# LSH attention with a token-mixing layer on one core: the order of issue as an explicit list

## The chip, the cores and the metric

One core of one Trainium2 chip runs the whole program. The metric is device time in microseconds (us). Five instruction streams run beside each other: PE (matrix multiply), DVE (VectorE), ACT (ScalarE), POOL (GpSimd) and SP, which here only issues DMAs. Each stream runs its instructions strictly in the order in which the program issued them, and waits on semaphores where it needs another stream's result.

## The reference

Attention with a hash mask comes first, and a token-mixing layer is put on its output:

```python
q_bucket = sum((q @ proj > 0) * 2**k)          # 6 hash bits, the same for k
scores   = where(q_bucket == k_bucket, q @ k.T / 8, -1e9)
attn     = exp(scores - rowmax); attn /= sum(attn) + 1e-9
x        = attn @ v                            # 4 batches, 8 heads, 768 tokens, 64 wide
theta    = x @ w_theta                         # x is now 4 x 768 x 512
y        = w_tok_r @ (x * cos(theta)) + w_tok_i @ (x * sin(theta))
u        = x + y
out      = u + relu(u @ w_ch)
```

Inputs are float32, and the three weight pairs come as float64.

## The kernel before

The kernel is cut into 3,785 small operations. An operation is a Python closure that issues a few instructions on one stream; it is made by `op(name, prio, alts, deps, slots)`, where `alts` names the streams that may run it, with a price in ns each. All matrix products are made of float16 halves (a high and a low part), so many operations exist only to split a tile: `qkh`/`qkl` (L643, L645, L649) for q and k, `p1`/`p2` (L879, L885) for the exponentials, `zh`/`zl` (L1095, L1097, L1101) for the rotated values, `xh`/`xl` (L1007, L1009, L1013) for x and u before they are turned by a DMA transpose (`xturn`, L1017).

For every head: `qkload` (SP) brings q and k, `qksq`, `qksum`, `qksc` find a scale, `qkh` and `qkl` split, `bits` (PE) and `sign` (DVE) make the hash rows, `assemble` and `assbits` (SP) copy the parts into the operands `qt` and `kt`. `qmax` (PE, tile sq) multiplies them once to find row maxima, which `vmax` (DVE, L793, tile mc) reads out of one of two PSUM banks; `vboth`, `mtr`, `row`, `put` write the maxima back into `qt`. Then `st` (PE) makes the masked scores, `pf` (ACT, L873) the exponentials, `p1` and `p2` the halves, and `pv` (PE, tile po) multiplies with v; `recip` and `norm` (L928, L934) write x.

For every batch, once its heads are done: six tiles of `xh`, `xl`, `xturn` and four `proj` on PE (tile ps_th), `turns`, `rest`, `mag`, then `trig` (ACT), `zf`, `zh`, `zl`; 72 `y` operations on PE (tile py); then for each of six token tiles `u`, `xh`, `xl`, `xturn`, four `proj` (tile ps_r), `relu`, `fin` (L1142) and `store` (SP, L1146). The weights are prepared beside the first batch (`wload`, `wlow`, `whigh`, `wmul` and others). The work of one batch's token mixing is interleaved with the next batch's attention; the last batch's stands alone at the end.

What sets the order: `issue_all()` (L117) sorts the operations by a rank (`prio` plus an offset per name and batch in `OFF`), hands out buffer slots by rank, and then runs a list scheduler. It keeps a simulated time per stream from the prices, takes the ready operation of the lowest rank for each idle stream, holds a stream back for an operation of a lower rank that is about to be ready (`HOLD`, `AHEAD`), and models the matrix clock, the DMA wire and the memory port that DVE and POOL share. Where `alts` has two streams, the one that is idle first in the simulation takes the operation. All of this happens when the program is built; the chip sees the resulting order on each stream alone.

Of the kernel before, what the change touches and what calls it, by code (L numbers as in the profile page):

```python
# [34 lines left out]
def lsh_attention_moe_kernel(ctx: ExitStack, tc: tile.TileContext, q, k, v, proj, w_theta, w_tok_r, w_tok_i, w_ch, aff, out):  # L35
# [46 lines left out]
    WINDOW = 3413  # L82
    SAME = {"PE": 0, "ACT": 120, "DVE": 115, "POOL": 160}
    START = {"PE": 1000, "ACT": 1900, "DVE": 1600, "POOL": 4300, "SP": 500}
    STREAM = {"xtr": 0.5, "wtr": 0.5, "mtr": 0.3, "vall": 0.3, "vmean": 0.5, "pv": 0.83, "y": 1.0, "proj": 0.97}
    FULLNS = 244
    LAT = {"PE": 220, "ACT": 120, "DVE": 115, "POOL": 140}
    SHARED = {"p1", "p2", "zf", "zh", "zl", "mag", "wlow", "whigh", "wmul", "wl", "vv2", "qkh", "qkl", "xh", "xl", "fin"}
    SHORT = {"pv", "xtr", "wtr", "mtr", "vall", "vmean", "bits"}
    FOUR = {"proj"}  # L90

# [25 lines left out]
    def issue_all():  # L117
        left = {}
        rng = random.Random(SEED)
        for i, o in enumerate(ops):  # L120
            o.key = (round(o.prio + JIT * rng.random(), 4), i)
            for sl in o.slots:
                left.setdefault(sl, []).append(o)

        free, done, open_, tickets = dict(FREE), set(), {}, {}

        def run(o):
            if o in done:
                return
            if o in open_:  # L130
                raise RuntimeError("no order for " + o.name)
            open_[o] = True
            for d in sorted(o.deps, key=lambda d: d.key):
                run(d)
            while True:
                need = {}
                for sl in o.slots:
                    if not sl.held:
                        need[sl.pool] = need.get(sl.pool, 0) + 1
                short = [p for p, n in need.items() if free[p] < n]  # L140
                if not short:
                    break
                held = [x for x in left if x.held and x.pool == short[0] and x not in o.slots]
                x = min(held, key=lambda x: max(u.key for u in left[x]))
                for u in sorted(left[x], key=lambda u: u.key):
                    run(u)
            for sl in o.slots:
                if not sl.held:
                    sl.held = True
                    free[sl.pool] -= 1  # L150
                    sl.rank = tickets[sl.pool] = tickets.get(sl.pool, -1) + 1
            done.add(o)
            del open_[o]
            for sl in o.slots:
                left[sl].remove(o)
                if not left[sl]:
                    free[sl.pool] += 1
                    del left[sl]

        for o in sorted(ops, key=lambda o: o.key):  # L160
            run(o)

        free = {p: list(range(n)) for p, n in FREE.items()}
        given = {p: set() for p in FREE}
        head = {p: 0 for p in FREE}
        busy = dict(START)
        wire = 0
        port = [0, 0]
        table = None
        succ = {o: [] for o in ops}  # L170
        avail = {e: [] for e in START}
        soon = {e: [] for e in START}
        for o in ops:
            for sl in o.slots:
                sl.held = False
            o.n = o.unissued = len(o.deps)
            o.at = 0
            for d in o.deps:
                succ[d].append(o)
            if not o.n:  # L180
                for e in o.alts:
                    avail[e].append(o)

        tail_pe = None

        def key(o, e):
            if e == "PE" and tail_pe in SHORT and o.name in FOUR:
                return (o.key[0] + PEN, o.key[1])
            return o.key

        def can(o):
            need = {}
            for sl in o.slots:
                if not sl.held:
                    if sl.rank - head[sl.pool] >= WIN.get(sl.pool, 1):
                        return False
                    need[sl.pool] = need.get(sl.pool, 0) + 1
            return all(len(free[p]) >= n for p, n in need.items())

        used, seen, warm = {}, 0, False  # L200

        def pace(t, dur, part):
            nonlocal seen, warm
            while (seen + 1) * WINDOW <= t:
                share = used.get(seen, 0) / WINDOW
                warm = share >= 0.75 or (warm and share > 0.43)
                seen += 1
            dur *= 1 if warm else 2
            a = t
            while a < t + dur:  # L210
                b_ = min(t + dur, (a // WINDOW + 1) * WINDOW)
                used[a // WINDOW] = used.get(a // WINDOW, 0) + (b_ - a) * part
                a = b_
            return dur

        events = [(t_, 0, []) for t_ in sorted(START.values())]
        now, todo, tick = 0, len(ops), 0
        while todo:
            progress = False
            for e in START:  # L220
                if busy[e] > now:
                    continue
                best = None
                for o in avail[e]:
                    k_ = key(o, e)
                    if best is not None and k_ >= best:
                        continue
                    end = now + (HOLD * o.alts[e][0] if e != "SP" else 0)
                    if any(x.at < end and key(x, e)[0] + AHEAD < k_[0] for x in soon[e]):
                        continue  # L230
                    if can(o):
                        best, pick = k_, o
                if best is None:
                    continue
                o = pick
                for a in o.alts:
                    avail[a].remove(o)
                for sl in o.slots:
                    if not sl.held:
                        p = sl.pool  # L240
                        sl.held = True
                        sl.idx = free[p].pop(0)
                        given[p].add(sl.rank)
                        while head[p] in given[p]:
                            given[p].remove(head[p])
                            head[p] += 1
                dur, fn = o.alts[e]
                lat = LAT.get(e, 0)
                if e == "PE":
                    if tail_pe in SHORT and o.name in FOUR:  # L250
                        dur += 80
                    tail_pe = o.name
                    dur = pace(now, dur, STREAM.get(o.name, 0.9))
                elif e == "DVE" and o.name in SHARED:
                    port[0] = max(now, port[1]) + dur
                    dur = port[0] - now
                elif e == "POOL":
                    port[1] = max(now, port[0]) + dur
                    dur = port[1] - now
                elif e == "SP":  # L260
                    t_ = now
                    for hold, size in dur:
                        t_ += 25 + hold
                        wire = max(wire, t_ + 650) + max(size / 360, 60)
                    dur = t_ - now
                    lat = wire + 1050 - t_
                if o.table is not None and o.table != table:
                    dur += 1280
                    table = o.table
                fn()  # L270
                busy[e] = now + dur
                if TRACE is not None:
                    TRACE.append((e, o.name, o.phase, now, dur))
                tick += 1
                same = [c for c in succ[o] if e != "SP" and list(c.alts) == [e]]
                o.same = same
                heapq.heappush(events, (now + dur + lat, tick, o))
# [11 lines left out]
            if progress:  # L289
                continue  # L290
# [1046 lines left out]
```

## Time and profile before

| | |
|---|---|
| runs | 761.12, 762.28, 764.10 us; median 762.28 |
| profiled execution | 763.9 us, span 762.1 us (first to last instruction) |
| busy PE / DVE / ACT / POOL | 705.0 / 582.8 / 550.2 / 409.4 us |
| mean granted TensorE clock | 0.986 of 2.4 GHz |

The span is 1.8 us shorter than the time of the same execution; the rest lies before the first and behind the last instruction. Busy time of PE counts overlapping matmuls once, so a PE that is busy is not always at its full rate. A wait is given as the stream and tile that waited and the one whose event ended it.

### The profile page before, as it was taken

What the parts mean: (1) busy time and instruction counts of PE and PEld (TensorE: products, weight loads), DVE (VectorE), ACT (ScalarE), POOL (GpSimd) and SP (SyncE); (2) the same over time, 40 slices, a digit from 0 to 9 for tenths busy, and PEclk for the clock granted to TensorE, in tenths of its full rate; (3) what the DMA queues carried; (4) which work ended last, traced back from release to release, by engine and by line L of the source; (5) the groups of instructions that cost most, each with busy time, mean ns of one, the idle gap of its engine ahead of it and who ended that gap; (6) DMA issues with size and microseconds to landing.
All of it is one profiled execution on the core that took longest, in us unless ns stands there. A gap on an engine that the chain in (4) does not pass through costs nothing.

```text
span 762.1 us, 17202 instructions
## 1 busy us (share of the span) xinstructions
PE 705.0 (93%) x6516; PEld 417.1 (55%) x6516; DVE 582.8 (76%) x1083; ACT 550.2 (72%) x970; POOL 409.4 (54%) x363
## 2 busy tenths in 40 slices
PE   3689999898899999989999999999999999989997
PEld 1266768674456545555555655565556555544443
DVE  6989988997999885887998755799988655468321
ACT  6478887788997667788896676788996655868111
POOL 3052451634776637776569666686579555733000
PEclk9699999999999999999999999999999999999999
DMA  6265534467103427435403332435204321151212
GB/s 221 86 193 195 164 98 135 94 169 150 40 15 103 111 53 160 118 95 112 77 25 84 92 93 67 125 86 139 64 25 101 80 62 32 29 98 28 56 33 78
DMA packets 85955, 72.09 MB, mean 95 GB/s; under 512 B 58144, under 2 KB 75632, under 8 KB 85872
## 3 DMA queue, kind: packets, MB, share of 16 engines
q1 hardware_dynamic: 85872, 70.99, 36.9%
q8 instruction: 51, 0.84, 0.5%
q14 instruction: 32, 0.26, 0.1%
HBM read 32.51 MB, written 6.29 MB: 51 GB/s over the span
## 4 chain that ended last, share of the span: by engine, by line
PE 54%; DVE 23%; ACT 9%; DMA 7%; issue 4%; POOL 2%; SPq 0%; DVEq 0%; ACTq 0%; POOLq 0%
PE py L79 20%; PE st L79 9%; PE po L79 9%; DVE mc L793 7%; PE ps_r L79 7%; PE sq L79 4%; PE ps_th L79 3%; DMA t_x<-s_x 2%; ACT pf L873 2%; ACT p L879 1%; POOL p L885 1%; DVE hl L649 1%; DMA w_th<-in_moe_w_theta_dram 1%; DMA t_u<-s_u 1%; DVE wf_t L394 1%
## 5 line engine op out<-in xcount | busy, mean ns | idle before, releaser
L885 POOL TENSOR_TENSOR p<-pf,p 128x512 f16<-128x512 f32 x252 | 315.6, 1276 | 190.0 <-ACT p L879 120.9
L793 DVE TENSOR_REDUCE mc<-sq 128x1 f32<-128x512 f32 (+1 forms) x288 | 187.6, 681 | 42.7 <-PE sq L79 41.9
L79 PE MATMUL py<-z,wtk 128*128 128x512 f16 x864 | 211.6, 379 | 1.0 <-POOL z L1101 0.6
L873 ACT ACTIVATE pf<-st 128x512 f32<-128x512 f32 x288 | 163.2, 592 | 58.3 <-PE st L79 45.3
L79 PE MATMUL st<-qt,kt 98*128 98x256 f16 (+3 forms) x768 | 167.4, 328 | 4.2 <-ACT pf L873 2.4
L879 ACT ACTIVATE p<-pf 128x512 f16<-128x512 f32 x252 | 151.0, 629 | 8.6 <-PE po L79 6.8
L79 PEld LDWEIGHTS <-p 128*128 128x128 f16 x3024 | 123.0, 98 | 40.5 <-issue 4.8
L79 PE MATMUL po<-vv,p 128*128 128x65 f16 x3024 | 132.9, 194 | 2.1 <-POOL p L885 1.6
L79 PEld LDWEIGHTS <-wtk 128*128 128x128 f16 x864 | 81.5, 98 | 87.2 <-issue 3.7
L79 PE MATMUL sq<-kt,qt 108*128 108x256 f16 (+1 forms) x384 | 105.0, 338 | 23.0 <-DVE mc L793 17.4
L79 PEld LDWEIGHTS <-kt 108*128 108x128 f16 (+1 forms) x768 | 70.9, 100 | 44.1 <-issue 12.4
L79 PE MATMUL ps_th<-wth,t_x 128*128 128x512 f16 x288 | 66.7, 379 | 5.2 <-DMA t_x<-s_x 5.2
L79 PE MATMUL ps_r<-wch,t_u 128*128 128x512 f16 x288 | 67.6, 379 | 2.7 <-DMA t_u<-s_u 2.3
L1101 POOL TENSOR_TENSOR z<-f,z 128x512 f16<-128x512 f32 x34 | 47.1, 1399 | 41.9 <-ACT z L1095 40.3
L79 PEld LDWEIGHTS <-qt 108*128 108x128 f16 x384 | 36.4, 102 | 57.7 <-issue 26.5
L1090 DVE SCALAR_TENSOR_TENSOR f<-x,zsc,z 128x512 f32<-128x512 f32 x48 | 53.1, 1143 | 2.2 <-ACT z L1078 1.2
L79 PEld LDWEIGHTS <-t_x 128*128 128x128 f16 x288 | 27.4, 98 | 38.7 <-DMA t_x<-s_x 7.5
L79 PEld LDWEIGHTS <-t_u 128*128 128x128 f16 x288 | 27.7, 98 | 35.6 <-DMA t_u<-s_u 3.3
L1129 DVE SCALAR_TENSOR_TENSOR x<-py,sw,x 128x512 f32<-128x512 f32 x24 | 17.9, 747 | 38.0 <-PE py L79 38.0
L1007 ACT ACTIVATE s_u<-x,su 128x512 f16<-128x512 f32 x18 | 13.0, 720 | 42.8 <-DVE x L1129 42.3
L649 DVE SCALAR_TENSOR_TENSOR hl<-raw,sc,hl 128x768 f16<-128x768 f32 x32 | 39.4, 1243 | 0.1
L79 PE MATMUL po<-vw,pf 128*128 128x65 f32 x288 | 36.9, 277 | 1.2 <-ACT pf L873 1.1
(163 smaller groups left out, 845.5 us busy)
## 6 DMA issues: line engine op xcount, KB each, us to landing
raw<-in_q_dram SPq DMA_DIRECT2D x16, 384.0 KB
raw<-in_k_dram SPq DMA_DIRECT2D x16, 384.0 KB
vb<-in_v_dram SPq DMA_DIRECT2D x16, 384.0 KB
out_dram<-x SPq DMA_DIRECT2D x24, 256.0 KB
qt<-hl SPq DMA_DIRECT2D x31, 192.0 KB
kt<-hl SPq DMA_DIRECT2D x31, 192.0 KB
w_t<-in_moe_w_tok_r_dram SPq DMA_DIRECT2D x6, 768.0 KB
w_t<-in_moe_w_tok_i_dram SPq DMA_DIRECT2D x6, 768.0 KB
```

The source lines that it names most:

```text
L79: PE.matmul(out_, l, r, start=start, stop=stop, skip_group_check=True)
L394: DVE.scalar_tensor_tensor(fu, t["hi"], 3, fu, ALU.logical_shift_left, ALU.bitwise_xor)
L649: DVE.scalar_tensor_tensor(t["hl"][:, 1, i], t["raw", i], t["sc"][:, 2 + i : 3 + i], t["hl"][:, 0, i], ALU.mult, ALU.subtract)
L793: DVE.tensor_reduce(col()[:, cs], u["sq"], AX.X, ALU.max)
L873: ACT.activation(wide("pf", spf, F32), u["st"], AF.Exp, scale=1.0 / (UNIT * math.sqrt(D)))
L879: ACT.activation(o_, u["pf"], AF.Copy)
L885: return lambda: eng.tensor_tensor(wide("p2", sp2, F16), u["pf"], u["p1"], ALU.subtract)
L1007: ACT.activation(u["s"][:, 0], src(), AF.Copy, scale=sc())
L1090: DVE.scalar_tensor_tensor(u["f"], tl[b][:, tt], zsc[:, b : b + 1], t["zw"][r][:, tt], ALU.mult, ALU.mult)
L1101: return lambda: eng.tensor_tensor(t["z"][r, 1][:, tt], u["f"], t["z"][r, 0][:, tt], ALU.subtract)
L1129: DVE.scalar_tensor_tensor(tl[b][:, to], res["py"], t["sw"][:, to : to + 1], tl[b][:, to], ALU.mult, ALU.add)
```

## The change

`issue_all()` no longer sorts or schedules. It goes through one list, `ORDER`, of 3,785 tokens, and issues the operations in just that order; `SLOTS` gives the buffer copy of each of the 2,010 slots. The ranks, `OFF`, the window and hold constants and the cost model are gone. Twenty or so prices in `alts` are changed too, but nothing reads a price any more.

```diff
     def issue_all():
-        left = {}
...
-        for o in sorted(ops, key=lambda o: o.key):
-            run(o)
...
+        seen = []
+        for o in ops:
             for sl in o.slots:
                 if not sl.held:
                     sl.held = True
...
+                    seen.append(sl)
+        for sl, c in zip(seen, SLOTS):
+            sl.idx = int(c)
+        done = set()
+        for line in ORDER.split():
+            e, x = line[0], int(line[1:], 36)
+            o = ops[x]
+            if not done.issuperset(o.deps):
+                raise RuntimeError("order of " + o.name)
             done.add(o)
...
+            o.alts[ENGINES[e]][1]()
...
-    proj_ready = op("pst", QK0, on("DVE", 700, split_proj), [cload])
+    proj_ready = op("pst", QK0, on("DVE", 1450, split_proj), [cload])
...
+ENGINES = {"P": "PE", "A": "ACT", "D": "DVE", "G": "POOL", "S": "SP"}
...
+P61 A9n D65 D1w P9q P66 A62 S9y P68 A1x D9r P9w D69 A9s D67 P6c A9u D9t P6a D6b Sdr D6d P6e A9z D9x P6g D6f Sa8 D6h P6i P6k D6j Ads D6l P6u
...
+P2uh P2vw P2vx P2vj P2vy D2vk P2vz D2uz A2vl P2w0 A2ui D2vm P2w1 P2w2 P2ts P2tt P2tu P2w3 A2tv S2v0 P2wi G2tw P2w4 S2ok S2p7 P2wj G2uj S2vn
+P2w5 P2wk P2wl P2v1 P2wm P2wn P2w6 P2wo D2w7 P2wp D2w8 P2wq P2wr P2ws P2wt P2v2 D2wu P2v3 D2wv P2v4 D2w9 P2vo D2ww S2wa P2vp P2vq P2vr A2vs
+S2wx A2v5 P2wb G2vt S2qh P2wc S2na P2wd S2vu P2we S2uk S2pu P2wy A2wf P2wz D2wg P2x0 D2v6 P2x1 S2v7 S2tx A2x2 S2wh D2x3 S2x4
```

A token is a stream's letter and the number of an operation, to base 36, in the order in which the program makes the operations. `A9u` is operation 354, the `qkh` of the second pair of heads, on ACT; `S2x4` is the last, 3784, a `store`.

The list is not the order that the old scheduler gives. Set beside the order in which the instructions stand in the trace of before, it keeps every operation and every buffer copy, but few operations keep their place:

| stream | operations before | in the list | places moved: median, nine in ten within, most |
|---|---|---|---|
| PE | 1460 | 1460 | 2, 8, 32 |
| DVE | 876 | 900 | 1, 5, 57 |
| ACT | 861 | 852 | 1, 5, 30 |
| POOL | 323 | 308 | 0, 1, 5 |
| SP | 265 | 265 | 1, 5, 32 |

Operations that change the stream: 21 `zl` and two `wmul` from POOL to DVE; 8 `zh`, 8 `xh`, 3 `mag` and 3 `qkh` from ACT to DVE; 4 `fin` from POOL to DVE. The other way 7 `qkh`, 5 `xh` and one `mag` go from DVE to ACT, and 10 `fin`, one `wmul` and one `zl` from DVE to POOL. On SP, nine stores are issued behind the last `xturn` (S2qh, S2na, S2vu, S2uk, S2pu, S2v7, S2tx, S2wh, S2x4); before, three were.

## Rows read from the trace of the kernel before

**Rows 1.** The page's first part: busy time of each engine, share of the span, instructions.
```profile
PE 705.0 (93%) x6516; PEld 417.1 (55%) x6516; DVE 582.8 (76%) x1083; ACT 550.2 (72%) x970; POOL 409.4 (54%) x363
```
**Rows 2.** Busy time of each engine by stage. Columns: stretch in us, its length, then busy us and instructions of PE, PE's weight loads, DVE, ACT and POOL, the granted clock, the busy share of the DMA engines, and GB/s.
```profile
0.00:17.00 17.00, 3.78 (x14) 1.54 (x15) 10.11 (x36) 11.50 (x16) 7.56 (x28) 1.00 0.71 230
17.00:50.00 33.00, 24.45 (x195) 12.71 (x196) 29.37 (x63) 21.43 (x39) 10.64 (x9) 0.79 0.48 139
50.00:165.00 115.00, 107.59 (x1120) 83.74 (x1119) 106.33 (x217) 91.23 (x172) 41.26 (x34) 1.00 0.47 137
165.00:220.00 55.00, 48.29 (x379) 24.84 (x378) 48.02 (x83) 49.23 (x82) 33.11 (x27) 1.00 0.43 94
220.00:300.00 80.00, 77.78 (x724) 44.25 (x723) 64.11 (x120) 56.73 (x114) 49.86 (x43) 1.00 0.40 95
300.00:340.00 40.00, 36.33 (x431) 22.40 (x428) 33.70 (x74) 32.11 (x61) 31.07 (x28) 1.00 0.42 111
340.00:390.00 50.00, 47.39 (x455) 27.47 (x455) 43.98 (x75) 42.03 (x70) 33.20 (x27) 0.97 0.38 80
390.00:500.00 110.00, 109.76 (x1092) 63.48 (x1089) 79.94 (x147) 79.05 (x144) 74.47 (x64) 1.00 0.35 89
500.00:545.00 45.00, 42.14 (x428) 25.36 (x425) 41.69 (x72) 40.77 (x70) 28.43 (x25) 0.96 0.48 110
545.00:660.00 115.00, 114.67 (x1142) 66.34 (x1141) 75.07 (x132) 81.51 (x144) 77.12 (x66) 1.00 0.22 54
660.00:695.00 35.00, 30.69 (x278) 17.16 (x277) 25.50 (x40) 27.23 (x42) 16.75 (x14) 1.00 0.36 68
695.00:757.60 62.60, 62.07 (x287) 27.81 (x285) 24.32 (x32) 16.73 (x25) 5.89 (x4) 1.00 0.19 47
757.60:762.10 4.50, 0.04 (x1) 0.00 (x0) 0.69 (x1) 0.69 (x1) 0.00 (x0) 0.86 0.15 58
```
**Rows 3.** What PE waited for over the whole span: waiting tile and line, what ended the wait, us in total, times, longest.
```profile
PE sq L79 <- DVE mc L793: 17.4, 34, 1.7
PE ps_th L79 <- DMA t_x<-s_x: 5.2, 5, 1.6
PE ps_r L79 <- DMA t_u<-s_u: 2.3, 2, 1.8
PE po L79 <- DVE x L934: 1.7, 1, 1.7
```
**Rows 4.** The page's chain of waits that ended last, by engine.
```profile
PE 54%; DVE 23%; ACT 9%; DMA 7%; issue 4%; POOL 2%; SPq 0%; DVEq 0%; ACTq 0%; POOLq 0%
```
**Rows 5.** PE's waits in one stretch each: 17 to 165 us, 165 to 220 us, 300 to 390 us (two rows), 660 to 695 us.
```profile
PE sq L79 <- DVE mc L793: 10.7, 17, 1.7
...
PE ps_th L79 <- DMA t_x<-s_x: 2.7, 2, 1.6
...
PE sq L79 <- DVE mc L793: 3.2, 8, 0.9
PE pmx L806 <- DVE mx L802: 1.7, 1, 1.7
...
PE ps_th L79 <- DMA t_x<-s_x: 2.1, 2, 1.5
```
**Rows 6.** Durations of operations that change the stream: from the groups by shape (count, busy us, mean ns, idle before), and from the answers on L1101 and on the tile x (count, min/median/max ns).
```profile
L645 DVE TENSOR_SCALAR hl<-raw,sc 128x768 f16<-128x768 f32 x11 | 8.3, 766 | 0.2
L1101 POOL TENSOR_TENSOR z<-f,z x34: 1155/1463/1617, 194.3 to 704.4; 128x512 f16<-128x512 f32 x34
L1101 DVE TENSOR_TENSOR z<-f,z x14: 692/997/1643, 195.3 to 707.3; 128x512 f16<-128x512 f32 x14
L1142 DVE TENSOR_TENSOR x<-rl,x x18: 679/693/1641, 283.3 to 758.5; 128x512 f32<-128x512 f32 x18
L1009 DVE TENSOR_SCALAR s_x<-x,zsc x10: 473/480/1382, 165.0 to 685.0; 128x512 f16<-128x512 f32 x10
L408 DVE TENSOR_TENSOR wf_ch<-wf_ch,wg_ch 128x256 f32<-128x256 f32 x3 | 3.0, 1000 | 1.3 <-ACT wf_ch L401 1.3
```
**Rows 7.** SP's stream in order of time: start, length and what it issued.
```profile
168.84 0.39 SPq L632 DMA_DIRECT2D raw<-in_k_dram  x1
169.31 2.21 SPq L1017 DMA_TRANSPOSE t_x<-s_x  x1
...
175.90 1.27 SPq L1017 DMA_TRANSPOSE t_x<-s_x  x1
```
**Rows 8.** DVE's stream in order of time, between 300 and 390 us (two rows) and between 660 and 695 us (a row with the idle time before it).
```profile
328.36 0.68 DVE L1142 TENSOR_TENSOR x<-rl,x 128x512 f32<-128x512 f32 x1
...
333.83 1.56 DVE L645 TENSOR_SCALAR hl<-raw,sc 128x768 f16<-128x768 f32 x1
...
670.57 0.18 DVE L928 RECIPROCAL rc<-po 128x4 f32<-128x4 f32 x1 [0.77 <-PE po L79]
```
**Rows 9.** The tail in order of time, and the last stretch (columns as in rows 2).
```profile
755.88 3.63 SPq L1146 DMA_DIRECT2D out_dram<-x  x2
...
758.46 0.69 DVE L1142 TENSOR_TENSOR x<-rl,x 128x512 f32<-128x512 f32 x1 [2.60 <-ACT rl L1139]
...
752.00:762.10 10.10, 5.11 (x23) 1.98 (x21) 2.08 (x3) 1.85 (x3) 0.00 (x0) 0.94 0.35 104
```

More of the change, by code (lines that the diff above doesn't have):

```diff
@@ L79, in mm @@
         PE.matmul(out_, l, r, start=start, stop=stop, skip_group_check=True)
[L82 to L90, printed above, removed]
     class Slot:
@@ L117, in issue_all @@
     def issue_all():
-        left = {}
[L119 to L146, printed above, removed]
+        seen = []
+        for o in ops:
             for sl in o.slots:
@@ L149, in run @@
                     sl.held = True
-                    free[sl.pool] -= 1
-                    sl.rank = tickets[sl.pool] = tickets.get(sl.pool, -1) + 1
-            done.add(o)
[L153 to L158, printed above, removed]
-        for o in sorted(ops, key=lambda o: o.key):
-            run(o)
-        free = {p: list(range(n)) for p, n in FREE.items()}
@@ L164, in issue_all @@
[L164 to L277, printed above, removed]
-                heapq.heappush(events, (now + dur, -tick, []))
-                if same:
-                    heapq.heappush(events, (now + dur + SAME[e], tick + 0.5, same))
-                for c in succ[o]:
-                    c.unissued -= 1
-                    c.at = max(c.at, now + dur + (SAME[e] if c in same else lat))
-                    if not c.unissued and len(c.alts) == 1:
-                        for a in c.alts:
-                            soon[a].append(c)
-                progress = True
-                todo -= 1
-            if progress:
-                continue
-            if not events:
-                raise RuntimeError("no order of issue: " + ", ".join(o.name for e in avail for o in avail[e])[:2000])
-            now = events[0][0]
-            while events and events[0][0] <= now:
-                _, _, o = heapq.heappop(events)
-                if isinstance(o, list):
-                    nexts = o
-                else:
-                    for sl in o.slots:
-                        sl.users -= 1
-                        if not sl.users:
-                            free[sl.pool].append(sl.idx)
-                    nexts = [c for c in succ[o] if c not in o.same]
-                for c in nexts:
-                    c.n -= 1
-                    if not c.n:
-                        for a in c.alts:
-                            avail[a].append(c)
-                            if c in soon[a]:
-                                soon[a].remove(c)
@@ L444, in prep_weight @@
         a = op("wall", last_, on("PE", 60, total), [a], [sa])
[L445 removed]
+        r = op("wcsc", last_, on("DVE", 620, lambda: root_scale(u["pa"], csc[nm], cinv[nm])), [a], [sa])
         for c in range(NC):
@@ L589, in prep_v @@
         r = op("vload", prio + LV0, on("SP", [(450, 2 * S * D * 4)], load), slots=[svb])
-        r = op("vsq", prio, on("ACT", 900, squares), [r], [svb, sv] + sw_)
+        r = op("vsq", prio, on("ACT", 950, squares), [r], [svb, sv] + sw_)
         r = op("vall", prio, on("PE", 60, total), [r], [svb, sa])
-        r = op("vscale", prio, on("DVE", 520, scale), [r], [sa])
+        r = op("vscale", prio, on("DVE", 630, scale), [r], [sa])
         vready[b].append(r)
-        last_ = a = op("vv1", prio, on("ACT", 960 if n_ == 1 else 830, high), [r], [svb, sv] + sw_)
+        last_ = a = op("vv1", prio, on("ACT", 1030 if n_ == 1 else 830, high), [r], [svb, sv] + sw_)
         if n_:
@@ L676, in prep_qk @@
         r = op("qksum", pr, on("PE", 60, total), sq, [sa, ssc])
-        r = op("qksc", pr, on("DVE", 850, scale), [r], [sa, ssc])
+        r = op("qksc", pr, on("DVE", 1260, scale), [r], [sa, ssc])
         for i, sn, high, low in parts:
@@ L978, in moe @@
         alltk = [o for w in wready["tk"] for o in w]
-        st0 = op("moe", G + at("TH0", b) - 0.5, on("DVE", 800 + 300, start), ([] if b == 0 else alltk) + vready[b] + wready["th"], sz)
+        st0 = op("moe", G + at("TH0", b) - 0.5, on("DVE", 2500 if b else 800, start), ([] if b == 0 else alltk) + vready[b] + wready["th"], sz)
         srow, st1 = [], st0
@@ L983, in moe @@
         if b == 0:
-            st1 = op("ssum", G + at("Y0", 0), on("DVE", 600, sums), [st0] + alltk)
-        st2 = op("sback", G + at("Y0", b), on("DVE", 300, back), [st1] + wready["ch"])
+            st1 = op("ssum", G + at("Y0", 0), on("DVE", 750, sums), [st0] + alltk)
+        st2 = op("sback", G + at("Y0", b), on("DVE", 400, back), [st1] + wready["ch"])
         cnt = [0]
@@ L1062, in mag_a @@
                     ACT.activation(t["zw"][0][:, tt], t["zw"][1][:, tt], AF.Abs)
-                a = op("turns", prio, on("ACT", 495, turns), [pe, st0], [sm_, s1])
-                d = op("rest", prio, on("DVE", 600, rest), [a, st0], [sm_, s1] + sz)
+                a = op("turns", prio, on("ACT", 590, turns), [pe, st0], [sm_, s1])
+                d = op("rest", prio, on("DVE", 650, rest), [a, st0], [sm_, s1] + sz)
                 angles.append((d, op("mag", prio, {"DVE": (335, mag), "ACT": (520, mag_a)}, [d], sz)))
@@ L1079, in go @@
                     ACT.activation(s_, s_, AF.Sin, scale=t["ns"])
-                tr = op("trig", prio, on("ACT", 220 + 844 * (t1 - t0), go), ang, sz, table="trig")
+                tr = op("trig", prio, on("ACT", 480 + 855 * (t1 - t0), go), ang, sz, table="trig")
                 for tt in range(t0, t1):
@@ L1206 @@
 GR = 0
-PEN = 2.584
 GR1 = 2
```

177 lines of the change are left out of this document (154 added, 23 removed), and 38 rows, old and new, of the table OFF.

## The prediction

> **What bounds the kernel now.** I began with the page's busy line: PE is busy for 705.0 of 762.1 us [rows 1], so at most 57.1 us can go by any order that keeps the work on PE as it is. The table by stage came next, because the share over the whole span hides where those 57 us lie [rows 2]. PE's idle time, stretch length less busy time, is 13.2 us up to 17 us, 8.6 from 17 to 50, 7.4 from 50 to 165, 6.7 from 165 to 220, 2.2 from 220 to 300, 6.3 from 300 to 390, 2.9 from 500 to 545, 4.3 from 660 to 695, and 4.5 in the tail. From 390 to 500, 545 to 660 and 695 to 757.6 it is 0.2, 0.3 and 0.5: there PE is the bound and no order helps. Third, PE's waits say what ended that idle time: the largest by far is qmax waiting for vmax to empty a PSUM bank, 17.4 us in 34 waits, then the DMA transposes t_x and t_u with 5.2 and 2.3 [rows 3]. Last, the chain of waits has 54% on PE, 23% on DVE and 9% on ACT [rows 4], which fits: outside PE's own stages DVE is the stream that sets the end. In 17 to 165 us DVE is itself busy for 135.7 of 148 us [rows 2].
>
> **The change part by part.** No PE operation is added or dropped, so a gain can come only from waits, from the granted clock, and from DVE work that leaves a stretch in which DVE is late. I go by stretch, and work against the profiled execution's own 763.9 us.
>
> 0 to 17 us: DVE runs without a gap between its first scale and the first vmax, and the list reorders the same operations on it. 0, and at most 1 either way.
>
> 17 to 165 us: of PE's 16.0 us idle, 10.7 are vmax [rows 5]. In this stretch the list takes three qkh from DVE to ACT (the first is A9u) and puts one back; at 0.77 each [rows 6] DVE has 1.5 us less to do ahead of the same PE operations. ACT has the room: it is busy for 112.7 of 148 us [rows 2]. The list also issues some vmax ahead of longer DVE work; I give that half a microsecond. -2.0; bounds 0 (the next operation on DVE is late instead) and -5, half of the vmax waits.
>
> 165 to 300 us: t_x costs PE 2.7 us [rows 5]. The second transpose took 2.21 us to issue behind two loads, the third 1.27 [rows 7]. The list puts the k load, 0.39 us of issue, behind the second and third transposes. 2.21 - 1.27 + 0.39 = 1.3; so -1.3, bounds 0 and -2.7. Against that, DVE gets five zl and two wmul from POOL and one xh from ACT, and gives up one wmul and two xh: 5 x 1.0 + 2 x 1.0 + 0.48 - 1.0 - 2 x 0.48 = 5.5 us [rows 6]. DVE's idle time there is 7.0 + 15.9 = 22.9 us [rows 2], and I cost this at nothing; if that cover fails it is the slower rival below.
>
> 300 to 390 us: vmax and vboth hold PE for 3.2 + 1.7 us [rows 5]. Two qkh go to ACT, one of them 1.56 us long, and a fin of 0.68 goes to POOL [rows 6, 8]: 0.77 + 1.56 + 0.68 = 3.0 us less DVE work. Two thirds of it stand in front of those waits: -2.0, bounds 0 and -4.9.
>
> 500 to 545 us: one more qkh leaves DVE, 0.77; -0.5, bounds 0 and -2.9, all of PE's idle time.
>
> The clock: the granted clock is 0.97 from 340 to 390 and 0.96 from 500 to 545 [rows 2], which is 1.5 and 1.8 us of PE time below the full level; both lie in stretches where PE has been pausing. Shorter pauses should keep about half of it: -1.5, bounds 0 and -3.3. That only these stretches and the start show a lower clock speaks for the connection and does not prove it.
>
> 660 to 695 us: PE waits 1.7 us for a norm [rows 3]. The list puts four PE operations (two pv, two st of the heads still running) in front of the pv that waits, which covers nearly all of it. But what follows, the first transposes of the last batch, hangs on DVE, and in DVE's stream only the 0.77 us before the next recip is free [rows 8]. Most of the 1.7 therefore comes back as a wait for t_x. Two stores that stood between the transposes leave for the tail, which should shorten the 2.1 us of t_x waits [rows 5] somewhat. -1.5, bounds 0 and -4.3.
>
> The tail: nine stores stand behind the last transpose, against three. In the last 10.1 us the DMA engines moved 104 GB/s at a busy share of 0.35, so about 297 GB/s when busy [rows 9]; nine stores of 262,144 bytes are then 7.9 us of transfers. The first can go out when seven PE operations are left; one is three matmuls, and 287 of these took 62.07 us before the end [rows 2], 0.65 us for three, so 7 x 0.65 = 4.5 us before PE ends, so the data end 3.4 us after PE. Before, the last fin ended at 759.15 [rows 9], the store went out at once and the span ended 2.9 us later; 0.9 of that is its data and 2.0 is fixed. The end comes 3.4 + 2.0 = 5.4 us after PE's, where it is 4.5 now. +0.9; bounds 0 (the transfers overlap with what is idle) and +3.5 (the first store only goes out three PE operations before the end). The Trainium skill, "DMA: Bandwidth & Descriptors", section "Queues, rings and completion order", says that each DMA engine consumes its descriptors in ring order. It speaks against the late stores, since the last one stands behind the data of eight others; by it the lower bound falls away. No row of before has more than a few stores in a row, so this is not shown here.
>
> The sum: -2.0 - 1.3 - 2.0 - 0.5 - 1.5 - 1.5 + 0.9 = -7.9, so 763.9 becomes 756.0. The profiled execution lies 1.6 us above the median of 762.28; on that scale the forecast is 754.4, written 754.5.
>
> **The rivals.** *The waits only move.* Most places differ by one or two, and where a producer is issued earlier something else on its stream is issued later. The stretch 660 to 695 shows how a wait of 1.7 us turns into another. For it: DVE's total work rises, and most waits are under a microsecond already. Against it: 1.5 and 3.0 us of DVE work really leave the stretches where vmax is late. Time: -7.9 shrinks to 0 to -3, with the tail's 0.9 in it: 759 to 763.
>
> *DVE becomes late between 165 and 264 us* (the slower side). The price is 5.5 us, and if the five zl run beside POOL at their longest, 1.64 instead of 1.0 [rows 6], 8.7. It decides if DVE's own idle time from 165 to 220, 7.0 us, is bound to inputs and cannot take the work; then y, proj and qmax slip together, and since PE is full from 390 on nothing is regained. The stretch 300 to 390 then gains nothing, because DVE arrives late. 762.3 - 2.0 + 8.7 + 0.9 = 769.9, say 770. Against it: PE was 97% busy from 220 to 300 with DVE at 80% [rows 2], and POOL's zl, at 1.46 us, was itself the slower way. The Trainium skill, "GPSIMD Engine Reference", section "Specifications", says that GpSimd shares its SBUF interfaces with DVE and contends with DVE instructions that have two SBUF inputs. The trace agrees as far as spreads go: zl runs from 0.69 to 1.64 us on DVE and from 1.16 to 1.62 on POOL; by that rule the upper price is the right one.
>
> *The order is better throughout.* Of the 57.1 us, 39.4 lie outside the start and the tail. If half of them goes, without new waits, the time is 742 to 743. For it: waits are many and small, the kind that local exchanges can cover. Against it: PE's places move by two in the median, and the DVE stretch before 165 us keeps nine tenths of its work.
>
> **How the numbers follow.** Forecast, 747 to 758.4: 0.50. Waits only move: 0.22. DVE late: 0.13. Better throughout: 0.15. A measurement of this kernel tells about 0.5% from no change, that is below 758.5 or above 766.1. Faster: 0.50 + 0.15 = 0.65; same 0.22; slower 0.13. The range of 744 to 765 holds the forecast's band, all of the second case, and a third of the last; about two in ten are left out. The forecast's own range is 747 to 758.4, near the sum of half of the bounds.
>
> **What would show it.** Right: vmax waits on PE in 17 to 165 us down from 10.7 to about 8.7, the t_x wait after 165 us halved, vmax and vboth waits in 300 to 390 below 3.5, the pv wait of 1.7 gone, the granted clock at 1.00 in both late stretches, and a tail a microsecond longer from the last matmul to the end. Wrong: PE idle in 220 to 300 above 5 us with DVE as its releaser; a PE idle sum that stays at 57; a tail over 7 us; or PE idle under 40.

## The result, and the profile after

The kernel with the list takes 738.53 us in the median of four runs (734.64 to 739.31), against 762.26 us: a ratio of 0.968, interval 0.964 to 0.972. That is 23.7 us faster. The sign was forecast; the size, 7.8 us, was a third of it, and 738.5 lies below the range. The profiled execution is the fastest of the four, 734.64 us with a span of 732.8, so the traces of the two kernels stand 29.3 us apart, 5.6 more than the medians. The accounts by stretch below go by the traces. Where one of a kernel's runs is over 1.5% longer than its fastest, the medians and ratios below leave that run out.

The page's first part and its chain of waits, after:

```profile
PE 695.1 (95%) x6516; PEld 415.4 (57%) x6516; DVE 556.8 (76%) x1107; ACT 546.3 (75%) x961; POOL 377.2 (51%) x348
...
PE 73%; DVE 16%; ACT 5%; issue 2%; DMA 2%; POOL 1%; SPq 1%; DVEq 0%; ACTq 0%; POOLq 0%
```

PE's idle time went from 57.1 to 37.7 us [rows 1], and the chain that ended last now runs on PE for 73% instead of 54% [rows 4]. The line to stop at is DVE's: it has 24 instructions more and is busy for 26.0 us less. More work in less time is what the rest of this section has to explain.

The busy time by stage, after. The columns are those of [rows 2]. Each stretch ends where PE has started as many of its 1,460 list entries as it had at the end of the matching stretch of before, so lengths compare row by row; which entries these are differs a little, so PE's instruction counts do too.

```profile
0.00:17.50 17.50, 3.75 (x14) 1.59 (x15) 10.71 (x37) 12.29 (x18) 7.55 (x28) 1.00 0.71 233
17.50:49.10 31.60, 25.25 (x205) 14.24 (x206) 28.03 (x60) 21.66 (x38) 12.42 (x9) 0.78 0.41 127
49.10:157.80 108.70, 104.87 (x1102) 82.93 (x1101) 101.86 (x214) 92.69 (x173) 38.85 (x34) 1.00 0.51 149
157.80:206.20 48.40, 46.79 (x385) 25.41 (x386) 45.29 (x90) 47.10 (x78) 25.59 (x21) 1.00 0.45 107
206.20:283.10 76.90, 76.75 (x715) 44.02 (x714) 58.40 (x119) 57.06 (x113) 44.21 (x41) 1.00 0.38 90
283.10:319.60 36.50, 35.97 (x440) 22.54 (x438) 29.50 (x70) 33.76 (x64) 29.47 (x27) 1.00 0.49 123
319.60:368.50 48.90, 45.67 (x445) 25.95 (x443) 42.04 (x80) 45.12 (x74) 32.05 (x28) 1.00 0.40 87
368.50:477.80 109.30, 109.30 (x1098) 63.74 (x1095) 78.51 (x153) 76.93 (x143) 70.64 (x62) 1.00 0.37 90
477.80:518.90 41.10, 40.28 (x441) 24.30 (x440) 35.07 (x69) 39.33 (x67) 24.53 (x22) 1.00 0.57 117
518.90:632.80 113.90, 113.90 (x1130) 66.02 (x1129) 77.34 (x144) 81.14 (x143) 68.03 (x60) 1.00 0.24 53
632.80:665.30 32.50, 30.41 (x276) 16.93 (x275) 26.28 (x44) 24.80 (x38) 17.43 (x14) 1.00 0.31 58
665.30:728.00 62.70, 62.10 (x288) 27.78 (x285) 23.04 (x35) 13.75 (x20) 6.47 (x5) 1.00 0.22 55
728.00:732.80 4.80, 0.03 (x1) 0.00 (x0) 0.69 (x1) 0.69 (x1) 0.00 (x0) 0.77 0.59 219
```

Length of before less length of after, beside my terms (the clock's 1.5 us lay in 300 to 390 and 500 to 545):

| stretch of before | forecast | traces | PE idle before, after |
|---|---|---|---|
| 0 to 17 | 0 | +0.5 | 13.2, 13.8 |
| 17 to 165 | -2.0 | -7.7 | 16.0, 10.2 |
| 165 to 300 | -1.3 | -9.7 | 8.9, 1.8 |
| 300 to 390 | -2.0 | -4.6 | 6.3, 3.8 |
| 390 to 500 | 0 | -0.7 | 0.2, 0.0 |
| 500 to 545 | -0.5 | -3.9 | 2.9, 0.8 |
| clock | -1.5 | in the stretches | |
| 545 to 660 | 0 | -1.1 | 0.3, 0.0 |
| 660 to 695 | -1.5 | -2.5 | 4.3, 2.1 |
| 695 to PE's end | 0 | +0.1 | 0.5, 0.6 |
| tail | +0.9 | +0.3 | 4.5, 4.8 |

With the clock's 1.5 us shared out by its 1.5 and 1.8, the stretches in which PE had pauses gave 1.7 times the forecast (300 to 390, 660 to 695), 3 times (500 to 545), 4 times (17 to 165) and 7 times (165 to 300). PE's waits over the whole span, after (columns as in [rows 3]):

```profile
PE sq L77 <- DVE mc L604: 8.5, 17, 1.7
PE pq L77 <- ACT hl L449: 5.9, 1, 5.9
PE sq L77 <- DVE kt L529: 5.3, 1, 5.3
PE pb L77 <- DVE pst_q L152: 2.5, 1, 2.5
PE ps_th L77 <- DMA t_x<-s_x: 2.3, 3, 1.5
PE st L77 <- ACT pf L684: 2.2, 6, 0.6
PE po L77 <- POOL p L696: 2.0, 4, 0.7
```

`vmax` went from 17.4 to 8.5 us, half its 34 waits; `t_x` from 5.2 to 2.3; `t_u` from 2.3 to 0.6. What is now longest, 5.9, 5.3 and 2.5, are three single waits that end by 17 us, in the start, which no exchange of later work touches.

Why DVE is busy for less shows in the groups by shape. The rows are the `zf`, `qkl`, `zl` and `vmax` (tile mc) of DVE, and `p2` of POOL; the columns are count, busy us, mean ns, idle before:

```profile
L901 DVE SCALAR_TENSOR_TENSOR f<-x,zsc,z 128x512 f32<-128x512 f32 x48 | 36.7, 792 | 1.8 <-ACT z L889 0.6 <-ACT z L890 0.6
L460 DVE SCALAR_TENSOR_TENSOR hl<-raw,sc,hl 128x768 f16<-128x768 f32 x32 | 34.5, 1086 | 1.4 <-ACT hl L454 1.0 <-DMA qt<-hl 0.2
L912 DVE TENSOR_TENSOR z<-f,z 128x512 f16<-128x512 f32 x34 | 27.7, 837 | 0.3
L604 DVE TENSOR_REDUCE mc<-sq 128x1 f32<-128x512 f32 x192 | 128.6, 683 | 33.5 <-PE sq L77 32.8
...
L696 POOL TENSOR_TENSOR p<-pf,p 128x512 f16<-128x512 f32 x252 | 307.4, 1238 | 235.7 <-ACT p L690 154.0 <-PE po L77 28.7 <-PE pa L77 19.6
```

DVE's rows of before, from the same view:

```profile
L1090 DVE SCALAR_TENSOR_TENSOR f<-x,zsc,z 128x512 f32<-128x512 f32 x48 | 53.1, 1143 | 2.2 <-ACT z L1078 1.2 <-POOL wf_ch L407 0.6 <-ACT z L1079 0.2
L649 DVE SCALAR_TENSOR_TENSOR hl<-raw,sc,hl 128x768 f16<-128x768 f32 x32 | 39.4, 1243 | 0.1
L1101 DVE TENSOR_TENSOR z<-f,z 128x512 f16<-128x512 f32 x14 | 15.1, 1076 | 1.1 <-ACT z L1095 0.9
L793 DVE TENSOR_REDUCE mc<-sq 128x1 f32<-128x512 f32 x192 | 126.6, 681 | 24.8 <-PE sq L79 24.6
```

The 48 `zf` are the same work in both kernels, and a mean one fell from 1143 to 792 ns, near the shortest of before (count, then shortest, median and longest in ns, from the view of the tile f of before):

```profile
L1090 DVE SCALAR_TENSOR_TENSOR f<-x,zsc,z x48: 737/1057/1649, 192.8 to 705.0; 128x512 f32<-128x512 f32 x48
```

Next to it, `zl` on DVE fell from 1076 to 837 while 20 more of them came. `mc`, which reads a PSUM bank and no SBUF tile, takes 681 to 683 in both. How an order can do that shows in the timeline of one passage of the first mixing, before (start, length, stream, operation, count):

```profile
192.78 2.06 DVE L1090 SCALAR_TENSOR_TENSOR f<-x,zsc,z 128x512 f32<-128x512 f32 x3
...
196.33 3.87 DVE L1090 SCALAR_TENSOR_TENSOR f<-x,zsc,z 128x512 f32<-128x512 f32 x3
...
194.26 3.16 POOL L1101 TENSOR_TENSOR z<-f,z 128x512 f16<-128x512 f32 x2 [2.97 <-ACT z L1095]
198.22 1.43 POOL L885 TENSOR_TENSOR p<-pf,p 128x512 f16<-128x512 f32 x1 [0.80 <-ACT p L879]
199.62 2.71 POOL L1101 TENSOR_TENSOR z<-f,z 128x512 f16<-128x512 f32 x2
```

Three `zf` took 2.06 us, 0.69 each, with POOL idle for all but the last 0.6 us of them (its row at 194.26 has 2.97 us of idle time before it); the next three, beside POOL's `zl` and `p2`, took 3.87, 1.29 each. The same passage, after:

```profile
184.47 1.42 DVE L901 SCALAR_TENSOR_TENSOR f<-x,zsc,z 128x512 f32<-128x512 f32 x2
...
186.33 1.28 DVE L604 TENSOR_REDUCE mc<-sq 128x2 f32<-128x512 f32 x2
...
188.60 0.75 DVE L901 SCALAR_TENSOR_TENSOR f<-x,zsc,z 128x512 f32<-128x512 f32 x1
189.26 0.69 DVE L912 TENSOR_TENSOR z<-f,z 128x512 f16<-128x512 f32 x1
...
185.62 1.28 POOL L696 TENSOR_TENSOR p<-pf,p 128x512 f16<-128x512 f32 x1 [1.28 <-ACT p L690]
186.86 1.16 POOL L912 TENSOR_TENSOR z<-f,z 128x512 f16<-128x512 f32 x1
190.09 1.16 POOL L912 TENSOR_TENSOR z<-f,z 128x512 f16<-128x512 f32 x1 [2.08 <-ACT z L906]
```

Here `zf` and `zl` of DVE fall for the most part into POOL's gaps (1.28 us before 185.62, 2.08 before 190.09), and while POOL works from 185.62 to 188.02, DVE has `mc` among others, two in 1.28 us. Between 157.8 and 283.1 us the twelve `zf` have a mean of 774 ns; between 165 and 300 of before it was 1117.

### The profile page after: what moved, and what is told of

It is laid out like the page before. It is cut to its first block, busy times and chain, and to the rows that moved or that the text cites. A ratio compares the mean times of both kernels' runs of the same rounds, so it can differ in the third digit from the quotient of the medians.

```text
span 732.8 us, 17132 instructions
## 1 busy us (share of the span) xinstructions
PE 695.1 (95%) x6516; PEld 415.4 (57%) x6516; DVE 556.8 (76%) x1107; ACT 546.3 (75%) x961; POOL 377.2 (51%) x348
## 4 chain that ended last, share of the span: by engine, by line
PE 73%; DVE 16%; ACT 5%; issue 2%; DMA 2%; POOL 1%; SPq 1%; DVEq 0%; ACTq 0%; POOLq 0%
PE py L77 25%; PE st L77 13%; PE po L77 13%; PE ps_r L77 7%; PE sq L77 6%; DVE mc L604 6%; PE ps_th L77 5%; PE pb L77 1%; ACT pf L684 1%; POOL p L696 1%; PE pm L77 1%; PE pwt L285 1%; ACT p L690 1%; DVE wf_t L215 1%; DVE wf_t L205 1%
## 5 line engine op out<-in xcount | busy, mean ns | idle before, releaser
L696 POOL TENSOR_TENSOR p<-pf,p 128x512 f16<-128x512 f32 x252 | 307.4, 1238 | 235.7 <-ACT p L690 154.0
L604 DVE TENSOR_REDUCE mc<-sq 128x1 f32<-128x512 f32 (+1 forms) x288 | 189.8, 683 | 49.5 <-PE sq L77 48.4
L77 PE MATMUL py<-z,wtk 128*128 128x512 f16 x864 | 209.3, 379 | 0.0
L77 PEld LDWEIGHTS <-p 128*128 128x128 f16 x3024 | 119.0, 97 | 33.4 <-POOL p L696 2.9
L77 PE MATMUL po<-vv,p 128*128 128x65 f16 x3024 | 128.7, 193 | 2.2 <-POOL p L696 2.0
L77 PE MATMUL sq<-kt,qt 108*128 108x256 f16 (+1 forms) x384 | 107.3, 335 | 14.5 <-DVE mc L604 8.5
L953 POOL TENSOR_TENSOR x<-rl,x 128x512 f32<-128x512 f32 x12 | 15.2, 1268 | 51.3 <-ACT rl L950 51.3
L912 POOL TENSOR_TENSOR z<-f,z 128x512 f16<-128x512 f32 x14 | 19.0, 1362 | 39.0 <-ACT z L906 28.7
L901 DVE SCALAR_TENSOR_TENSOR f<-x,zsc,z 128x512 f32<-128x512 f32 x48 | 36.7, 792 | 1.8 <-ACT z L889 0.6
L77 PEld LDWEIGHTS po<-vw,pf 128*128 128x128 f32 x288 | 36.0, 192 | 2.1 <-ACT pf L684 0.6
```

The lines of the kernel that those rows point to most:

```text
L77: PE.matmul(out_, l, r, start=start, stop=stop, skip_group_check=True)
L604: DVE.tensor_reduce(col()[:, cs], u["sq"], AX.X, ALU.max)
L696: return lambda: eng.tensor_tensor(wide("p2", sp2, F16), u["pf"], u["p1"], ALU.subtract)
L901: DVE.scalar_tensor_tensor(u["f"], tl[b][:, tt], zsc[:, b : b + 1], t["zw"][r][:, tt], ALU.mult, ALU.mult)
L912: return lambda: eng.tensor_tensor(t["z"][r, 1][:, tt], u["f"], t["z"][r, 0][:, tt], ALU.subtract)
L953: return lambda: eng.tensor_tensor(tl[b][:, to], v_["r"], tl[b][:, to], ALU.add)
```

## The experiments

The first question was which part carries the gain: the form as a list, the order, the changes of stream, or one stream's order by itself. Theory **J** says that the streams' orders fit one another and pay only together. Later came **C**, much of the gain is DVE and POOL work that no longer stands beside each other, against **W**, it is waits that are covered, and shorter operations are a by-product. An exchanged pair below is two operations of one stream whose order differs between the two kernels. Diffs of the list show one line of several.

**The old order as a list.** The list and the loop of the new kernel, with the order and streams read from the trace of before.

```diff
-S5c S5e S0 S5v A5d S1u A5f P5g D5h D1 A5i A5k D5j P5m A5w D5l P5x D5o S9m A5p S9o D5r S6s D5y A5q D5n A5z A5t D5u D5s A9p S6t D60 P64 D1v
+S5c S5e S5v S0 A5d S1u A5f P5g A5w D5h P5x D1 A5i D5y P5m A5k D5j A5z D5l D5n S9m A5p S9o S6s A5q D5o D5r D5s A5t D5u D60 A9n P64 D1v P61
```

> The order and the streams of before, written out as the explicit list. Both theories: the form of the list does nothing by itself, so 760 to 765 us and PE idle near 57 us. A time under 755 would mean that something besides the order has changed.

Measured: 762.63 us, ratio 1.000 (0.997 to 1.004). Issuing from a list changes nothing. Both lists also give every slot the same buffer copy, so only the order and the streams in the list are left.

**Order and streams apart.** The new list with all 74 changes of stream undone (the expectations count 61), and the old order with all of them made. The first, from the new list (`A9u`, a `qkh`, back on DVE):

```diff
-P61 A9n D65 D1w P9q P66 A62 S9y P68 A1x D9r P9w D69 A9s D67 P6c A9u D9t P6a D6b Sdr D6d P6e A9z D9x P6g D6f Sa8 D6h P6i P6k D6j Ads D6l P6u
+P61 A9n D65 D1w P9q P66 A62 S9y P68 A1x D9r P9w D69 A9s D67 P6c D9u D9t P6a D6b Sdr D6d P6e A9z D9x P6g D6f Sa8 D6h P6i P6k D6j Ads D6l P6u
```

> The new list, but the 61 operations that changed their stream run on the old one, at their place in the list. Theory O (the order alone covers the waits): 738 to 745 us, DVE busy well below 582 us all the same. Theory S (taking zl and wmul off POOL frees DVE, whose two-input instructions were stretched beside POOL's): 750 to 758 us, DVE busy 575 us or more.

> The old order, with the 61 operations moved to their new streams at their old places. Theory O: no gain or a loss, 758 to 768 us, since DVE takes more work at unchanged places. Theory S: 745 to 755 us, DVE busy about 560 us, the mean zf on DVE near 0.8 us instead of 1.14.

Measured: the new order on the old streams 750.84 us (ratio 0.985, 0.979 to 0.990), the old order on the new streams 769.81 (1.011, 1.007 to 1.014). So the order alone gives 11 us, the changes of stream alone cost 8, and together they give 24: once the order is there, the same changes bring 12. DVE, with the same 1,083 instructions as before, is busy for 550.4 us under the new order, 32.4 less than before:

```profile
PE 700.8 (94%) x6516; PEld 416.5 (56%) x6516; DVE 550.4 (74%) x1083; ACT 550.1 (73%) x970; POOL 396.2 (53%) x363
```

Neither theory is right as it stood. The first time lies in S's range, but DVE's busy time is what O had said. In the second kernel a mean `zf` falls to 920 ns, two thirds of the way to S's 0.8 us, and the kernel is 8 us slower all the same; PE waits longer for `vmax` than before, 21.1 against 17.4:

```profile
PE sq L77 <- DVE mc L604: 21.1, 40, 1.8
...
L901 DVE SCALAR_TENSOR_TENSOR f<-x,zsc,z 128x512 f32<-128x512 f32 x48 | 42.8, 920 | 1.1 <-ACT z L889 0.6 <-ACT z L890 0.4
```

**One part of the changes of stream at a time**, undone in the new list: `zl` and `wmul` (23 operations); then the 35 between ACT and DVE; then the 14 `fin`. The first, one line:

```diff
-P27x S286 A3z D28i Ppk D28f Pra A28j Prr So3 Ppf Arb D40 P27y D28l A28g P27z D28k Apg G28h P280 Drc Drs Ps5 D28r Apl Ppp Aph P287 D28o Apq
+P27x S286 A3z D28i Ppk D28f Pra A28j Prr So3 Ppf Arb G40 P27y D28l A28g P27z D28k Apg G28h P280 Drc Drs Ps5 D28r Apl Ppp Aph P287 D28o Apq
```

> The new list with only the 21 zl and two wmul put back from DVE to POOL. Theory O: within 3 us of the new kernel, 737 to 742 us. Theory S: most of what e1 loses is lost here too, 747 to 756 us, and the mean zf on DVE is back above 1.0 us.

> The new list with the 35 operations that changed between ACT and DVE (qkh, xh, zh, mag) put back on their old streams; zl, wmul and fin stay on the new ones. Together with the run that put back zl and wmul, all moves undone cost 12.3 us. If the ACT and DVE exchange carries the rest: 745 to 750. If fin carries it, or if only the whole set matters: 739 to 743.

> The new list with the 14 fin that changed streams put back. If fin's places matter little, as fin feeds only the stores: 738 to 741. If fin carries the rest of the moves' worth, because it sits in DVE's stream in front of operations that PE waits for: 744 to 749.

Measured: 741.04, 745.48 and 741.59 us (ratios 0.971, 0.978 and 0.973; intervals of half a per cent either way). Against 738.53 they are 2.5, 7.0 and 3.1 us slower; the sum, 12.6, meets the 12.3 of all at once (these three leave out one `zl` and one `wmul`, which went from DVE to POOL). Only the 7.0 of the ACT and DVE exchange stands clearly off the uncertainty of a run, and it was forecast; the 3.1 of `fin` lies between its two forecasts. With `zl` and `wmul` back on POOL a mean `zf` takes 886 ns, so what S expected of that run did not come. Taking `zl` to DVE, which I had priced as the danger, is worth no loss here.

**One stream's order at a time.** The old order and streams, with one stream's operations put in the new order as far as operands and buffers allow: PE (2,951 of its 3,089 exchanged pairs), DVE (1,173 of 1,183), SP (298 of 311), and DVE, ACT and POOL together. PE's, against the old order's list:

```diff
-S5c S5e S5v S0 A5d S1u A5f P5g A5w D5h P5x D1 A5i D5y P5m A5k D5j A5z D5l D5n S9m A5p S9o S6s A5q D5o D5r D5s A5t D5u D60 A9n P64 D1v P61
+S5c S5e S5v S0 A5d S1u A5f P5g A5w D5h D1 A5i P5m A5k D5j P5x D5y A5z D5l D5n S9m A5p S9o S6s A5q D5o D5r D5s A5t D5u D60 A9n D1v P64 P61
```

> Old streams; PE in the new order (2951 of 3089 exchanged pairs), the other streams in the old one but for under a tenth of their pairs. Theory P (PE's order covers the waits): 752 to 757 us. Theory J (the orders only pay together): 759 to 768 us, and the wait of qmax for vmax not below 15 us.

> Old streams; DVE in the new order (1173 of 1183 pairs), the others old. Theory D (DVE serves PE's next need first): 751 to 757 us, and the wait of qmax for vmax near 9 us. Theory J: 759 to 768 us.

> Old streams; SP's DMAs in the new order (298 of 311 pairs), all else old. Theory T (transposes ahead of loads and stores): 755 to 758 us, PE's waits for t_x and t_u from 7.5 us to under 4. Otherwise: 760 to 764 us.

> Old streams; DVE, ACT and POOL in the new order, PE and SP old. Theory D: 751 to 756 us, nearly all of what the order gives with the old streams (750.8 us). Theory J: 757 us or more.

Measured: 867.76, 874.39, 795.83 and 911.33 us: 106, 113, 34 and 150 us slower than the 761.39 of before beside them, far outside what I expected; P, D and T all fail. Places that move by two in the median are not small when only one side moves. PE's waits with the new order on DVE, ACT and POOL alone:

```profile
PE sq L77 <- DVE mc L604: 48.4, 45, 3.6
PE po L77 <- POOL p L696: 27.2, 19, 6.4
PE st L77 <- ACT pf L684: 23.9, 26, 2.0
```

The producers and PE now ask for the same results in different orders, and all three kinds of wait grow several times over, `vmax` from 17.4 to 48.4 us. DVE is busy for only 552.8 us in this kernel, 30.0 less than before, so shorter work on DVE does not by itself make the program faster. Theory J has the direction right, and the size is far beyond what it had claimed.

**POOL's work taken away from beside DVE.** `p2` computed for 64 of 512 columns, in the old order and in the new:

```diff
+    p2s = [const.tile([P, 512], F16, name=f"p2c{n}") for n in range(BUFS["p2"])]
+    for p2_ in p2s:
+        DVE.memset(p2_, 0.0)
...
-                    return lambda: eng.tensor_tensor(wide("p2", sp2, F16), u["pf"], u["p1"], ALU.subtract)
+                    def go():
+                        u["p2"] = p2s[sp2.idx]
+                        eng.tensor_tensor(u["p2"][:, :64], u["pf"][:, :64], u["p1"][:, :64], ALU.subtract)
+                    return go
```

> This kernel has the old order as a list, with p2 (the low half of the exponentials, on POOL) computed for only 64 of its 512 columns, the rest held at zero: 7/8 of that low half is left out. Both theories: POOL's busy time falls by some 60 us or more, DVE's zf (mean 1.14 us in the old order) falls towards 0.75. Theory C (a good part of the 24 us between the two orders is DVE and POOL work that runs longer because the two stand beside each other): the old order gains most, 745 to 753. Theory W (the 24 us are waits that the new order covers, and the longer durations are a by-product): 758 to 763, since PE waits for the same producers.

> The new list with the same narrowed p2, the same 7/8 of the low half left out. Theory C: 734 to 738, close to the new list itself, so that the two orders stand 10 to 15 us apart. Theory W: 734 to 741, still about 20 us or more below the old order narrowed in the same way.

Measured: 747.30 us (0.982, 0.975 to 0.988) and 731.89 (0.961, 0.955 to 0.967). The old order gains 14 on the 761.48 beside it, the new 7 on 738.53; the two stand 15 us apart instead of 24. That is between the theories, and it could still be PE's waits for `p2` that went. So the next pair keeps all of POOL's work and takes only that wait away.

```diff
-                        u["p2"] = p2s[sp2.idx]
-                        eng.tensor_tensor(u["p2"][:, :64], u["pf"][:, :64], u["p1"][:, :64], ALU.subtract)
+                        u["p2"] = p2s[0]
+                        eng.tensor_tensor(p2w[sp2.idx], u["pf"], u["p1"], ALU.subtract)
```

> The old order as a list; POOL computes p2 over all 512 columns as before, but into tiles that nobody reads, and PE takes a tile of zeros in its place: the low half of the exponentials is left out of the result, PE's work is the same, and no PE operation waits for p2. Theory C (what the narrow p2 saved, 14 us, came from DVE operations that no longer ran beside POOL): 757 to 762, with zf's mean above 1.0 us. Theory W (it came from PE no longer waiting for p2, directly or through the buffers): 745 to 751, with zf's mean still above 1.0 us.

> The new list with p2 computed in full and not read, the low half left out of the result as in the run before it. Theory C: 735 to 739, like the new list itself. Theory W: 731 to 735, like the new list with the narrow p2.

Measured: 762.02 us (0.998, 0.994 to 1.002) and 736.04 (0.966, 0.961 to 0.972). Without its waits for `p2` the old order is where it was. The DVE and POOL groups of the old order with `p2` unread, and then with 64 columns:

```profile
L907 DVE SCALAR_TENSOR_TENSOR f<-x,zsc,z 128x512 f32<-128x512 f32 x48 | 53.1, 1142 | 2.2 <-ACT z L895 1.2 <-POOL wf_ch L218 0.6 <-ACT z L896 0.2
...
L701 POOL TENSOR_TENSOR p2c<-pf,p 128x512 f16<-128x512 f32 x252 | 315.9, 1278 | 185.9 <-ACT p L693 180.8 <-DVE vv L362 2.9 <-DVE vinv L177 1.8
```

```profile
L907 DVE SCALAR_TENSOR_TENSOR f<-x,zsc,z 128x512 f32<-128x512 f32 x48 | 43.5, 939 | 5.4 <-POOL z L918 3.2 <-ACT z L895 1.2 <-POOL wf_ch L218 0.6
...
L701 POOL TENSOR_TENSOR p2c<-pf,p 128x64 f16<-128x64 f32 x252 | 93.4, 374 | 357.3 <-ACT p L693 236.7 <-issue 44.9 <-PE st L77 31.2
```

With POOL's `p2` at 315.9 us a `zf` takes 1142 ns whether anyone reads `p2` or not; at 93.4 us it takes 939. DVE's busy time falls by 52.7 us with the narrow `p2` in the old order (582.6 to 529.9) and by 25.3 in the new one (557.0 to 531.7). Between these two pairs the old order gains 14.7 us and the new one 4.2. So of the 26.0 us between the orders with `p2` unread, 10.6 go when POOL's `p2` work goes; by the ratios it is 8, and the four intervals together leave some 8 us either way, so little more than the sign of that figure is certain. Theory C may hold for about two fifths of the gain, and not for all: 15.4 us are left between the orders with the narrow `p2`, where DVE is busy for nearly the same time in both. What these runs don't part is DVE's shorter operations from POOL's other work starting earlier, or from ACT getting back sooner the buffers that `p2` reads (its `pf` waits 7.7 us for `p2` with `p2` unread, 5.8 with 64 columns).

**One stretch at a time.** The new list up to PE's operation 285 and the old from there; and the new list only between operations 285 and 530. The first line of the first kernel that differs from the new list:

```diff
-Aog Goc Dnn Po8 Aoz Dnp Svf Pnq A3s Goh Dnr Aok Pns Pod A270 D3q Pp3 Aol Poo D271 Ap4 Pnu Gom Dnt S272 Aop Dr1 Pnw Ap0 Pot D3r Aoq Sre Poi
+Aog Goc Dnn Po8 Aoz Dnp Svf Pnq A3s Goh Dnr Aok Pns A270 D271 Pp3 Aol Pod Dr1 Svh D3q Ap4 Poo S272 Gom Ap0 Poi Pp8 Aop Dnt Pnu Sre Pot Gp1
```

> The new list up to PE's operation 285 (about 165 us), from there the old order and the old streams. If the new order's gain is made where it is seen, stage by stage: about 7 us, 753 to 757. If the early gain lives from what the list does later, or is given back when the old order takes over: 759 to 764. If the early order brings the late gain too: below 748.

> The new list only between PE's operations 285 and 530 (about 165 to 297 us), the old order and streams before and behind. If stage by stage: about 9 us, 751 to 756. If it is given back: 759 to 764. My prediction's term for this stretch was 1.3 us, which would be 760 to 762.

Measured: 754.29 us (0.990, 0.984 to 0.996) and 755.12 (0.990, 0.987 to 0.993), 8.3 and 7.5 us faster than the 762.61 beside them. Each gain is what the traces show for its own stretch, and it is kept when the old order takes over. The second says in one number how far off my term was: 7.5 us (5 to 10 by the interval) where I had 1.3.

## Why the prediction was wrong in size

*The step that failed first* is the sentence that opened the second part: a gain "can come only from waits, from the granted clock, and from DVE work that leaves a stretch". There is a fourth source, DVE work that stays and takes less time. I took each duration from one trace as a property of the operation, although [rows 6] gave `zl` a spread of 0.69 to 1.64 us and `fin` one of 0.68 to 1.64, and although I named POOL as its cause, in the slower rival only. In that rival the spread was a price that the change might pay. It did not occur to me that a new order could stop paying it: DVE's busy time fell by 32.4 us with the same instructions, before any operation changed its stream. In 17 to 165 us it fell from 135.7 to 129.9 us with the whole change, where I had taken off 1.5. What this is worth in time is less sure: some 10 of the 26 us between the orders went with POOL's `p2`, and the rest is the order of all streams together, not divided further. The Trainium skill, "GPSIMD Engine Reference", section "Specifications", says that GpSimd's SBUF interfaces are shared with VectorE, with contention for DVE instructions that have two SBUF inputs. The traces agree: `zf`, which reads two SBUF tiles, goes from 1142 to 939 ns as POOL's `p2` shrinks, and `mc`, which reads PSUM, stays within 681 to 684.

*165 to 300 us, -1.3, measured -9.7 in the traces and -7.5 alone.* Mis-sized, by its upper bound already: I took 2.7, the `t_x` waits, where PE's idle time in that stretch was 8.9. It held other waits too, this one among them, before:

```profile
PE ps_r L79 <- DMA t_u<-s_u: 1.8, 1, 1.8
```

PE's waits there, after:

```profile
PE po L77 <- POOL p L696: 0.7, 1, 0.7
PE sq L77 <- DVE mc L604: 0.4, 2, 0.2
PE st L77 <- ACT pf L684: 0.4, 1, 0.4
```

No wait for `t_x` or `t_u` is left. The 5.5 us more for DVE "costed at nothing" were paid for by DVE itself: it is busy for 103.7 us there, against 112.1, with 209 instructions against 203 [rows 2].

*17 to 165 us, -2.0, measured -7.7, and -8.3 alone.* Mis-sized, past its bound of 5. The `vmax` waits fell to 7.2 us where I had 8.7 [rows 5], so that part came out a little better than forecast; PE's idle time fell by 5.8 us in all. I went by one named wait, and "half a microsecond" for the reordering was a guess without a row. PE's longest there, after:

```profile
PE sq L77 <- DVE mc L604: 7.2, 12, 1.7
```

*300 to 390 us, -2.0, measured -4.6; 500 to 545 us, -0.5, measured -3.9; the clock, -1.5.* The granted clock is 1.00 in both stretches after, so all of the 1.5 and 1.8 us came back, the clock term's bound and not half of it. Waits for `vmax` and `vboth` from 300 to 390 are 0.4 and 0.2 us, well below the 3.5 that was to show the step right. Here the mechanism was right and the size short.

*660 to 695 us, -1.5, measured -2.5.* The 1.7 us wait of `pv` is gone, as worked out, and one `t_x` wait of 1.5 us is left.

*The tail, +0.9, measured +0.3.* PE's end to the end of the span went from 4.5 to 4.8 us. In that last stretch the stores moved 219 GB/s where before it was 58 [rows 2]: nine stores close together cost little more than three, nearer to my lower bound. The span ends 3.3 us after the last `fin`, against 2.9 before, so the eight stores in front of the last one held it up by some 0.3 us. The mis-sized term is the 3.4 us of data behind PE's end; with the 2.0 us that I took as fixed it was 2.8.

*The rivals.* "DVE becomes late" has the wrong sign with the new order: undoing `zl` and `wmul` makes it 2.5 us slower, if anything. In the old order the changes of stream do cost 8 us, so the danger was real for a list that moves operations without re-ordering round them. "The waits only move" cost time only in the start, where one wait (tile pb) grew from 1.1 to 2.5 us. "The order is better throughout" was it, and with the working I gave: half of 39.4 us was to go, and PE's idle time outside start and tail is 37.7 - 13.8 - 4.8 = 19.1. It still fell 4 us short, because PE's busy time also fell by 9.9 us, of which the clock explains 3.3; matmul means are the same to 1%, and the rest is left open. I gave it 0.15 since "places move by two in the median". That argument fails by the runs: the same small moves cost 34 to 150 us on one side alone, and gave 11 on all sides together with the old streams.

Of the signs named ahead, PE idle "under 40" was one of those that would show me wrong, and it did: 37.7.

## What to carry to other kernels

Before you price a re-ordering, look at the spread of one operation's duration in the trace (shortest, median, longest). Where the mean stands far above the shortest, part of the duration may hang on what runs beside it, and so on the order. The sum of mean less shortest, here 48 x (1.143 - 0.737) = 19 us for `zf` alone, bounds what a new order can take off that stream. It is no forecast of the kernel's time: with the changes of stream alone `zf` fell to 920 ns and the kernel became 8 us slower. Bound each stretch by all the idle time of the engine that limits it, not by the one wait whose cure you see. And judge a new order whole: moves between engines that cost 8 us in one order bring 12 in another, and one stream's order without the others' is no measure of it.

## What had not been expected of the hardware

A DVE operation with two SBUF tiles ran 1.9 times as long beside POOL (three `zf` at 0.69 and three at 1.29 us, 4 us apart in one trace), while `mc`, which reads PSUM, did not change. And streams that each run strictly in order suffered much from a small mismatch: the new order on PE alone, with no work added and places that move by two in the median, made the kernel 14% slower.
